# Score groups in neighbouring PSUM banks, chosen by age, and FFN outputs two units into the next block

## The chip, the cores and the metric

The kernel runs on one NeuronCore of a Trainium2 chip. The metric is the device time of one execution in microseconds, inputs in HBM to output in HBM; times are given as medians of several runs. The engines are named as the profile names them: PE (matmuls and transposes; PEld is its weight load), DVE, ACT, POOL and SP, which here only issues DMAs.

## The reference

Causal attention with a few "beacon" keys ahead of the sequence, then a feed-forward network whose hidden layer is the maximum of three products:

```python
B, H, S, Nb, D = 8, 8, 576, 16, 64
k_all = concatenate([beacon_k, k], axis=2)            # 592 keys, beacons always seen
v_all = concatenate([beacon_v, v], axis=2)
scores = q @ k_all.transpose(0, 1, 3, 2) / sqrt(D)    # masked where key is later than query
a = exp(scores - max); a /= a.sum(-1) + 1e-9
x = (a @ v_all).transpose(0, 2, 1, 3).reshape(B * S, H * D)     # 4608 x 512
h = maximum(maximum(x @ w1, x @ w2), x @ w3)          # 512 -> 768
out = h @ w_out                                       # 768 -> 512
```

All inputs and the output are float32 in HBM; the kernel computes in bfloat16 with float32 sums.

## The kernel before

The 64 heads (8 batches of 8) are worked on as 32 pairs of heads. Two pairs make a quad; two quads make a batch. The program's order is written out by hand, so each engine runs its instructions in the order in which the code emits them. Pairs 0 to 7 are emitted step by step (`first_steps` and the loop over `PPB` to `FIRST_BURST`), with PSUM banks in fixed roles. From pair 8 on each pair is one round, and all eight PSUM banks form one ring: `next_bank` takes the bank that was taken longest ago and puts it at the ring's end. This ring is where the change acts.

A round of pair p emits, in order:

- `emit_burst(p)`: the scores of both heads in four groups of matmuls (L510). Keys are the stationary side and queries the moving one; the two heads of a group go to two banks, and one exponential on ACT (L528) reads both banks and writes the tile `at_sb` in bfloat16. A burst takes all eight banks.
- In even rounds, `emit_pv_whole` for the quad of the two pairs before: the sums and the product with v (L628) into four banks. ACT copies the product to `raw` (L638, L639) and makes the reciprocal of the sums by a logarithm and an exponential (L644 to L646).
- The causal masks of this pair's `at_sb`, on POOL (L550).
- Five or six FFN units. A unit of the first product (`mm1_unit`, L703) makes 128 hidden channels of 512 tokens for one of the three weights, four matmuls into one bank, and DVE copies it (L720) or takes the maximum with what is there (L722). A unit of the output (`mm2_unit`, L750) makes 128 tokens of the output, six matmuls into one bank, and DVE copies it to `y` (L757). The last unit of a round (`close`) is cut into two halves in two banks. After the first unit, in rounds up to pair 14, stands the turn of the next pair: transposes of q and k on PE (L387) into two banks, copied by ACT (L423) and DVE (L434). Later pairs are turned by transposing DMAs instead (L379, L380). After the second unit come the plan's steps: casts of k, q and v from float32 on POOL (L260, L303), loads, stores.
- In even rounds at the end, `finish`: DVE multiplies `raw` by the reciprocal into two rows of `xT` (L651), which the first product reads.

Stores of output (L782), loads and transposing DMAs are all issued by SP, which takes them in order.

The FFN's blocks of 512 tokens are listed ahead in `units`: 18 units of the first product, then four of the output, for nine blocks. A unit may be emitted when its tokens' attention has been finished (`need` against `ready`). What is left after pair 31 runs at the end: three units, the last product, two units, the last `finish`, then the rest.

The two banks of a score group are the next two of the ring, sorted; the exponential reads them as a view with their distance as step (L522, L530):

```python
lo, hi = sorted(next_bank() for _ in range(2))
...
    in_=acc[:, lo : hi + 1 : hi - lo, 0 : g_width(p, gi)],
```

Of the kernel before, what the change touches and what calls it, by code (L numbers as in the profile page):

```python
# [16 lines left out]
def kernel(  # L17
# [23 lines left out]
    TOKB = 512  # L41
# [18 lines left out]
    PPB = H // 2  # L60
# [20 lines left out]
    NG = len(groups_any)  # L81
# [11 lines left out]
    def groups(p):  # L93
        if p < PPB:
            return groups_0
        return groups_any if p < FIRST_WHOLE else groups_whole

    def g_width(p, gi):
        return sum(q1 - q0 for _, q0, q1 in groups(p)[gi])
# [34 lines left out]
    N_BANK = 8  # L134
    acc = psum.tile([128, N_BANK, 512], FP32, name="acc")
# [18 lines left out]
    free_banks = list(range(N_BANK))  # L154

    def next_bank():
        i = free_banks.pop(0)
        free_banks.append(i)
        return i

    def next_psum(dtype=FP32):
        view = acc[:, next_bank()]
        return view if dtype == FP32 else view.bitcast(dtype)
# [32 lines left out]
    def pv_bank(i, dtype=FP32):  # L196
        return pv_psum[i].tile(dtype)
# [186 lines left out]
    def turn(p, i, ps):  # L384
        src = stage.pop(("pair16", p, i))
        for r in range(QR):
            nc.tensor.transpose(  # L387
                ps[:, r * QP : (r + 1) * QP],
                src[:, r].rearrange("p h d -> p (h d)"),
                ident[0:QP, 0:QP],  # L390
            )
# [30 lines left out]
    def evac_q(p, ps, copy):  # L422
        copy(  # L423
            qTs[p % NT].rearrange("d (p r) -> d p r", r=QR),
            ps.rearrange("d (r p) -> d p r", r=QR),
        )
# [5 lines left out]
    def evac_k(p, ps, copy):  # L432
        kT = kTs[p % NT]
        copy(  # L434
            kT[:, Nb:NK].rearrange("d (p r) -> d p r", r=QR),
            ps.rearrange("d (r p) -> d p r", r=QR),
        )
# [8 lines left out]
    def turn_pair(p, q_copy, spare="pv"):  # L446
        if spare == "any":
            banks = [next_psum(BF16) for i in range(2)]
        elif spare == "sc":
            ps = sc_psum.tile(BF16)  # L450
            banks = [ps[:, i] for i in range(2)]
        else:
            banks = [pv_bank(i, BF16) for i in range(2)]
        banks = [bank[:, 0:S] for bank in banks]
        for i in range(2):
            turn(p, i, banks[i])
        evac_k(p, banks[1], by_dve)
        evac_q(p, banks[0], q_copy)
# [21 lines left out]
    def both_heads(p, gi):  # L480
        W = g_width(p, gi)
        x0 = g_base(p, gi)
        return at[p][:, x0 : x0 + 2 * W].rearrange("k (e c) -> k e c", e=2)
# [24 lines left out]
    def score(p, t, e, q0, q1, ps):  # L508
        hs = slice(64 * e, 64 * e + 64)
        nc.tensor.matmul(  # L510
            ps,
            kTs[p % NT][hs, 128 * t : 128 * t + 128],
            qTs[p % NT][hs, q0:q1],
            start=True,
            stop=True,
            tile_position=(64 * e, 0),
        )

    def emit_burst(p):
        at[p] = at_pool.tile([128, AT_W], BF16, name="at_sb")  # L520
        for gi in range(NG):
            lo, hi = sorted(next_bank() for _ in range(2))  # L522
            off = 0
            for t, q0, q1 in groups(p)[gi]:
                for e in range(2):
                    score(p, t, e, q0, q1, acc[:, (lo, hi)[e], off : off + q1 - q0])
                off += q1 - q0
            nc.scalar.activation(  # L528
                out=both_heads(p, gi),
                in_=acc[:, lo : hi + 1 : hi - lo, 0 : g_width(p, gi)],  # L530
                func=AF.Exp,
                scale=scale,
            )
# [251 lines left out]


    units = []
    for tb in range(n_tokb):
        need = 2 * ((TOKB * (tb + 1) - 1) // S) + 1
        if tb == 0:  # L790
            for n, lo in ((0, 0), (need, MID)):
                for i in range(2):
                    for ft in range(0, n_ft, 2):
                        units.append((n, mm1_halves, (tb, ft, i, lo, lo + MID)))
        for i in range(2 if tb == 0 else 0, 3):
            for ft in range(n_ft):
                units.append((need, mm1_unit, (tb, ft, i)))
        for tt in range(TOKB // 128):
            units.append((need, mm2_unit, (tb, tt)))
    END = len(units)  # L800
    UPB = END // n_tokb
    done = [0]
# [5 lines left out]
    def emit_ffn(limit, new_ps=ffn_psum.tile, close=False):  # L808
        if not may_emit(limit):
            return False  # L810
        need, fn, args = units[done[0]]
        done[0] += 1
        fn(*args, new_ps, *([True] if close else []))
        return True
# [75 lines left out]
    def steps(p):  # L890
        return [[0, 1], [2, 3]]
# [55 lines left out]
    for b in range(2, B):  # L947
        p = b * PPB
# [5 lines left out]
    for b in range(B_PE, B):  # L954
        p = b * PPB
# [9 lines left out]
    def emit_all():  # L965
        start()
        for group, fns in first_steps:
            if group:
                emit_scores(*group)
            for fn in fns:  # L970
                fn()
        first = done[0]
        n_step = 0
        n_y = 0
        for p in range(PPB, FIRST_BURST):
            for s, gs in enumerate(steps(p)):
                for gi in gs:
                    emit_scores(p, gi)
                for gi in gs:
                    emit_masks(p, gi)  # L980
                for args in pv_at.pop((p, s), ()):
                    emit_pv(*args)
                    invert_sums()

                n_step += 1
                allowed = first + n_step * (UPB - first) / N_FIRST
                if s == 0:
                    turn_pair(p + 1, by_act, "pv" if p < PPB + 2 else "sc")
                    emit_ffn(allowed)
                    place_beacons(p + 1, by_act)  # L990
                    store_y(n_y)
                    n_y = len(y_out)
                    for fn in plan.pop((p, s), ()):
                        fn()
                    emit_ffn(allowed)
                    n_y = len(y_out)
                    emit_ffn(allowed)
                    multiply()
                else:
                    emit_ffn(allowed)  # L1000
                    multiply()
                    store_y(n_y)
                    n_y = len(y_out)
                    for fn in plan.pop((p, s), ()):
                        fn()
                    emit_ffn(allowed)
                    n_y = len(y_out)
                while emit_ffn(allowed):
                    pass
        v_tiles.pop(0)  # L1010

        for p in range(FIRST_BURST, NPAIR):
            b, pi = divmod(p, PPB)
            emit_burst(p)
            finish = emit_pv_whole(p // 2 - 1) if p % 2 == 0 else None
            for gi in range(NG):
                emit_masks(p, gi)
            n_step += 2
            if n_step <= N_FIRST:
                allowed = first + n_step * (UPB - first) / N_FIRST  # L1020
            else:
                allowed = UPB + (n_step - N_FIRST) * UPB / (2 * PPB)
            n = 0
            while may_emit(allowed):
                n_y = len(y_out)
                emit_ffn(allowed, next_psum, not may_emit(allowed, 1))
                store_y(n_y)
                n += 1
                if n == 1 and p + 1 < B_PE * PPB:
                    turn_pair(p + 1, by_act, "any")  # L1030
                    place_beacons(p + 1, by_act)
                if n == 2:
                    for fn in plan.pop((p, 0), ()):
                        fn()
            assert n >= 2
            if finish:
                finish()
            for s in range(2):
                for fn in plan.pop((p, s), ()):
                    fn()  # L1040
            if pi == 0:
                v_tiles.pop(b - 1)
        assert not plan and not loads and not pv_at
        for _ in range(3):
            emit_ffn(END, next_psum)
        finish = emit_pv_whole(NPAIR // 2 - 1)
        for _ in range(2):
            emit_ffn(END, next_psum)
        finish()
        store_y(len(y_out))  # L1050
        while emit_ffn(END - 1, next_psum):
            store_y(len(y_out))
        mm2_last(n_tokb - 1, TOKB // 128 - 1, (0, 320, 512))

    with tc.manual_schedule():
        emit_all()
# [30 lines left out]
```

## Time and profile before

| | |
|---|---|
| median of 3 runs | 329.25 us (324.11, 329.25, 329.5) |
| profiled execution | 325.05 us, span 323.3 us |
| mean granted PE clock | 0.973 |
| PE busy | 288.2 us (89%) |
| DVE, ACT, POOL busy | 182.0, 150.0, 132.9 us |
| stretch of bursts | about 58.7 to 261.8 us |
| FFN alone, after the last product | from 271.1 us |

The span is from the first to the last instruction. A wait is put down to the one that came last of what an instruction waited for, and the time in the chain of waits follows the work that ended last back to the start. A line number is that of the kernel before; in a helper all callers share it. The granted clock is given as a share of full speed.

### The profile page before, as it was taken

How to read it: one execution, taken by the hardware profiler on the slowest of the kernel's cores; microseconds unless marked ns; L12 is line 12 of the kernel's file. 1: busy time of each engine (PE TensorE's matmuls, PEld its weight loads, DVE VectorE, ACT ScalarE, POOL GpSimd, SP SyncE). 2: the span in 40 equal slices, each digit the busy share in tenths (PEclk: the TensorE clock that was granted, in tenths of full speed). 3: DMA queues.
4: the chain of work that ended last, by engine and by line, in shares of the span. 5: the costliest groups of instructions: out<-in, count | busy, mean ns of one | idle time of the engine just before them, and what ended most of it. 6: DMA issues, size and time to landing. Idle time of an engine off the chain costs nothing.

```text
span 323.3 us, 8611 instructions
## 1 busy us (share of the span) xinstructions
PE 288.2 (89%) x3539; PEld 165.1 (51%) x3539; DVE 182.0 (56%) x330; ACT 150.0 (46%) x247; POOL 132.9 (41%) x253
## 2 busy tenths in 40 slices
PE   7789969996997979968997889987998899999995
PEld 4557645554563445525553477744554455444442
DVE  4746724470946529433745437562945395776873
ACT  3775755866474274634674245547464733000000
POOL 6274674656284744462461635374225220000000
PEclk9999989997999899979998999999999999999999
DMA  8999999999864599979989699938502000301103
GB/s 153 189 178 254 216 250 265 207 299 233 211 153 90 122 277 222 151 156 253 279 182 162 161 275 205 193 110 177 113 2 97 34 2 2 130 3 65 65 1 132
DMA packets 85320, 50.67 MB, mean 157 GB/s; under 512 B 64416, under 2 KB 80032, under 8 KB 85280
## 3 DMA queue, kind: packets, MB, share of 16 engines
q1 hardware_dynamic: 80672, 45.76, 61.8%
q0 software_dynamic: 4048, 4.03, 7.5%
q8 instruction: 27, 0.44, 0.6%
q10 hardware_dynamic: 560, 0.33, 0.4%
q14 instruction: 13, 0.11, 0.1%
HBM read 35.13 MB, written 14.22 MB: 153 GB/s over the span
## 4 chain that ended last, share of the span: by engine, by line
PE 73%; ACT 9%; DMA 6%; POOL 4%; issue 3%; DVE 3%; SPq 1%; ACTq 0%; POOLq 0%; DVEq 0%
PE acc L703 39%; PE acc L750 13%; PE acc L628 10%; ACT at_sb L528 7%; PE acc L510 5%; DMA st<-in_v_dram 3%; DMA quad<-in_k_dram 2%; ACT at_sb L504 2%; POOL v_sb L303 2%; PE acc L387 1%; PE acc L594 1%; DVE hT L722 1%; POOL p L260 1%; PE acc L495 1%; SPq L222 1%
## 5 line engine op out<-in xcount | busy, mean ns | idle before, releaser
L703 PE MATMUL acc<-xT,w_sb 128*128 128x512 bf16 (+1 forms) x732 | 136.5, 342 | 0.0
L528 ACT ACTIVATE at_sb<-acc 128x416 bf16<-128x416 f32 (+1 forms) x96 | 76.1, 867 | 87.1 <-PE acc L510 56.1
L550 POOL TENSOR_SCALAR_AFFINE_SELECT at_sb<-at_sb 128x256 bf16<-128x256 bf16 (+2 forms) x148 | 58.9, 411 | 116.5 <-ACT at_sb L528 98.8
L703 PEld LDWEIGHTS <-w_sb 128*128 128x128 bf16 x732 | 69.8, 98 | 57.8 <-issue 0.8
L722 DVE TENSOR_TENSOR hT<-hT,acc 128x512 bf16<-128x512 bf16 (+1 forms) x114 | 69.8, 630 | 38.7 <-PE acc L703 36.1
L750 PE MATMUL acc<-w_out_sb,hT 128*128 128x512 bf16 (+1 forms) x246 | 53.4, 369 | 4.0 <-ACT at_sb L528 2.6
L720 DVE CAST hT<-acc 128x512 bf16<-128x512 f32 (+1 forms) x54 | 33.0, 630 | 41.5 <-PE acc L703 35.3
L260 POOL CAST p<-st 96x768 bf16<-96x768 f32 x56 | 44.4, 822 | 0.4 <-DMA st<-in_k_dram 0.4
L757 DVE COPY y<-acc 128x512 f32<-128x512 f32 (+1 forms) x41 | 25.1, 613 | 31.6 <-PE acc L750 16.3
L750 PEld LDWEIGHTS <-hT 128*128 128x128 bf16 x246 | 24.0, 102 | 29.0 <-issue 7.7
L510 PE MATMUL acc<-qT,kT 64*128 64x80 bf16 (+4 forms) x288 | 25.1, 282 | 13.1 <-ACT at_sb L528 12.5
L504 ACT ACTIVATE at_sb<-acc 128x992 bf16<-128x992 f32 (+6 forms) x32 | 26.3, 863 | 13.1 <-PE acc L495 13.0
L510 PEld LDWEIGHTS <-kT 64*128 64x128 bf16 x288 | 12.8, 94 | 27.4 <-issue 22.2
L628 PE MATMUL acc<-at_sb,v_sb 128*32 128x80 bf16 (+5 forms) x936 | 24.2, 249 | 0.0
L775 ACT COPY y<-acc 128x320 f32<-128x320 f32 x1 | 0.4, 425 | 46.3 <-PE acc L768 46.3
L651 DVE TENSOR_TENSOR xT<-raw,recip 128x576 bf16<-128x576 f32 x26 | 20.7, 838 | 0.0
L303 POOL CAST v_sb<-st 128x1536 bf16<-128x1536 f32 (+2 forms) x21 | 18.3, 893 | 1.5 <-DMA st<-in_v_dram 1.5
L638 ACT COPY raw<-acc 128x496 f32<-128x496 f32 x26 | 14.2, 597 | 9.5 <-PE acc L628 9.5
L628 PE MATMUL acc<-at_sb,ones 128*32 128x80 bf16 (+5 forms) x468 | 14.2, 248 | 5.0 <-ACT at_sb L528 5.0
L628 PEld LDWEIGHTS <-v_sb 128*32 128x32 bf16 (+1 forms) x936 | 16.2, 100 | 4.3 <-issue 0.2
L434 DVE COPY kT<-acc 128x576 bf16<-128x576 bf16 x12 | 9.0, 753 | 9.1 <-ACT kT L430 5.1
L731 PE MATMUL acc<-xT,w_sb 128*128 128x256 bf16 x96 | 13.0, 285 | 0.8 <-DVE qT L423 0.6
(65 smaller groups left out, 172.7 us busy)
## 6 DMA issues: line engine op xcount, KB each, us to landing
out_dram<-y SPq DMA_DIRECT2D x35, 256.0 KB, 2.1
st<-in_q_dram SPq DMA_DIRECT2D x28, 288.0 KB, 5.3
st<-in_k_dram SPq DMA_DIRECT2D x28, 288.0 KB, 6.1
st<-in_v_dram SPq DMA_DIRECT2D x24, 256.0 KB, 5.8
w_sb<-in_moe_w_dram POOLq DMA_DIRECT2D x6, 384.0 KB, 6.7
q_dram<-p SPq DMA_DIRECT2D x16, 144.0 KB, 2.3
k_dram<-p SPq DMA_DIRECT2D x16, 144.0 KB, 2.2
st<-in_v_dram SPq DMA_DIRECT2D x8, 224.0 KB, 5.5
```

The lines of the kernel that those rows point to most:

```text
L260: cast(t16.rearrange("p r h d -> p h r d"), st[0:QP, i * NQ2 : (i + 1) * NQ2].rearrange("p (h r d) -> p h r d", h=2, r=QR),)
L303: cast(v_sb[0:n, t:t1].rearrange("p t h d -> p (t h d)"), st[0:n, (t - t_lo) * H * D : (t1 - t_lo) * H * D],)
L504: nc.scalar.activation(out=both_heads(p, gi), in_=ps[:, :, 0 : g_width(p, gi)], func=AF.Exp, scale=scale)
L510: nc.tensor.matmul(ps, kTs[p % NT][hs, 128 * t : 128 * t + 128], qTs[p % NT][hs, q0:q1], start=True, stop=True, tile_position=(64 * e, 0),)
L528: nc.scalar.activation(out=both_heads(p, gi), in_=acc[:, lo : hi + 1 : hi - lo, 0 : g_width(p, gi)], func=AF.Exp, scale=scale,)
L550: nc.gpsimd.affine_select(out=view, in_=view, compare_op=ALU.is_ge, fill=0.0, base=x0, pattern=[[0, 2], [1, hi - lo]], channel_multiplier=-1,)
L628: nc.tensor.matmul(acc[32 * j : 32 * j + 32, bank, lo + q0 - qa : lo + qb - qa], lhsT, at_view(PPQ * quad + j // 2, t, j % 2, q0, qb), sta ...
L703: nc.tensor.matmul(ps[:, a:b], w_in[i][:, ct, 128 * ft : 128 * (ft + 1)], xT[:, ct, x0 : x0 + b - a], start=(ct == 0), stop=(ct == n_ct - 1),)
L720: by_dve(h[:, lo:hi], ps[:, lo:hi])
L722: nc.vector.tensor_max(h[:, lo:hi], h[:, lo:hi], ps[:, lo:hi])
L750: nc.tensor.matmul(ps[:, lo:hi], hT[:, ft, 128 * tt : 128 * (tt + 1)], w_out_sb[:, ft, lo:hi], start=(ft == 0), stop=(ft == n_ft - 1),)
L757: nc.vector.tensor_copy(y[:, lo:hi], ps[:, lo:hi])
```

## The change

Score groups: `next_pairs` puts the four aligned pairs of banks (0 and 1, 2 and 3, ...) in order by the later place that either bank has in the ring, and makes the ring those pairs in that order. The four groups of a burst take the pairs one after the other, and the exponential reads two neighbouring banks.

FFN order: the four output units of a block stand behind the first two units of the next block. Block 0 keeps its outputs at its own end, and so does the last one.

In pair 6 one FFN unit is emitted ahead of the next pair's turn instead of behind it.

```diff
+    def next_pairs():
+        pairs = sorted(
+            range(0, N_BANK, 2), key=lambda i: max(free_banks.index(i), free_banks.index(i + 1))
+        )
+        free_banks[:] = [i + j for i in pairs for j in range(2)]
+        return pairs
...
-        for gi in range(NG):
-            lo, hi = sorted(next_bank() for _ in range(2))
+        for gi, first in enumerate(next_pairs()):
             off = 0
             for t, q0, q1 in groups(p)[gi]:
                 for e in range(2):
-                    score(p, t, e, q0, q1, acc[:, (lo, hi)[e], off : off + q1 - q0])
+                    score(p, t, e, q0, q1, acc[:, first + e, off : off + q1 - q0])
                 off += q1 - q0
             nc.scalar.activation(
                 out=both_heads(p, gi),
-                in_=acc[:, lo : hi + 1 : hi - lo, 0 : g_width(p, gi)],
+                in_=acc[:, first : first + 2, 0 : g_width(p, gi)],
...
     units = []
+    outputs = []
     for tb in range(n_tokb):
         need = 2 * ((TOKB * (tb + 1) - 1) // S) + 1
+        blocks = []
...
         for i in range(2 if tb == 0 else 0, 3):
             for ft in range(n_ft):
-                units.append((need, mm1_unit, (tb, ft, i)))
-        for tt in range(TOKB // 128):
-            units.append((need, mm2_unit, (tb, tt)))
+                blocks.append((need, mm1_unit, (tb, ft, i)))
+        units += blocks[:2] + outputs + blocks[2:]
+        outputs = [(need, mm2_unit, (tb, tt)) for tt in range(TOKB // 128)]
+        if tb == 0:
+            units += outputs
+            outputs = []
+    units += outputs
...
                 if s == 0:
+                    if p == PPB + 2:
+                        emit_ffn(allowed)
                     turn_pair(p + 1, by_act, "pv" if p < PPB + 2 else "sc")
-                    emit_ffn(allowed)
+                    if p != PPB + 2:
+                        emit_ffn(allowed)
```

## The prediction

> **What bounds the kernel now.** I read the page first (shares, chain), then the waits of PE, then the chain in order of time, and last the granted clock in short windows.
>
> ```profile
> span 323.3 us, 8611 instructions
> PE 288.2 (89%) x3539; PEld 165.1 (51%) x3539; DVE 182.0 (56%) x330; ACT 150.0 (46%) x247; POOL 132.9 (41%) x253
> PE 73%; ACT 9%; DMA 6%; POOL 4%; issue 3%; DVE 3%; SPq 1%; ACTq 0%; POOLq 0%; DVEq 0%
> ```
>
> PE is the bound: 288.2 of 323.3 us, and 73% of the chain. So the change is worth what it takes out of PE's idle time, or out of the time that PE's own work lasts. Who makes PE wait:
>
> ```profile
> PE acc L510 <- ACT at_sb L528: 12.5, 8, 2.0
> PE acc L628 <- ACT at_sb L528: 5.0, 2, 2.5
> PE acc L750 <- ACT at_sb L528: 2.6, 1, 2.6
> PE acc L750 <- DVE hT L722: 1.4, 5, 0.3
> ```
>
> Columns: total us, times, longest. The first three rows are one thing: 8 + 2 + 1 = 11 waits, 20.1 us, all for an exponential (L528) of a burst. A burst is one head pair's scores: four groups of matmuls, each into two banks, each group read by one exponential. There are 24 bursts (pairs 8 to 31). One burst that waits, and one that doesn't (us from the start, us, what):
>
> ```profile
> 101.45 0.67 PE L510 MATMUL acc<-qT,kT 64*128 64x208 bf16 x6
> 104.10 0.43 PE L510 MATMUL acc<-qT,kT 64*128 64x336 bf16 x6 [1.98 <-ACT at_sb L528]
> 91.65 0.94 PE acc L510 x11
> 92.59 2.27 PE acc L628 x108
> ```
>
> In the burst at 101.45 the fourth group (336 columns wide at its first piece) starts 1.98 us late, released by an exponential. The burst at 91.65 takes 0.94 us and PE goes straight into the attention product.
>
> The rotation of banks says which bursts wait. Each burst begins at some place in a ring of eight banks; between bursts the kernel takes one bank for each FFN unit, a second for the last unit of the round, two for a turn, four for a product. Counted through the program, the start is odd in pairs 10, 13, 14, 17, 18, 21, 22, 25, 26, 29 and 30: eleven. With an odd start one group gets banks 7 and 0, and its view is acc[:, 0:8:7], whose reach covers all eight banks. In the instruction order of the kernel before, the matmul into bank 1 that follows carries a wait for that exponential, though it reads only 0 and 7. Eleven odd starts, eleven waits.
>
> The waits cost a second time. Where PE's granted clock was down in this stretch:
>
> ```profile
> 77.01:80.42 3.41, 3.41 (x91) 2.33 (x84) 0.00 (x0) 2.05 (x5) 1.25 (x2) 0.50 1.10 212
> 104.32:107.73 3.41, 3.41 (x22) 1.64 (x19) 0.44 (x1) 1.01 (x2) 2.27 (x5) 0.50 0.00 0
> 141.86:145.27 3.41, 3.41 (x10) 1.17 (x9) 0.69 (x1) 0.00 (x0) 3.41 (x6) 0.50 0.64 171
> 176.00:179.41 3.41, 3.31 (x13) 1.34 (x13) 0.00 (x0) 1.05 (x2) 1.99 (x4) 0.50 0.33 101
> 141.65 1.69 PE L750 MATMUL acc<-w_out_sb,hT 128*128 128x512 bf16 x4 [2.56 <-ACT at_sb L528]
> 141.65 5.73 PE acc L750 x18
> 314.40 3.88 PE acc L750 x18
> ```
>
> The value after the five engines is the clock: 0.50 for 3.41 us, four times, each within a microsecond of the end of one of the long waits. Eighteen output matmuls take 5.73 us after the wait at 141.65, against 3.88 us at the end of the kernel: 1.85 us lost.
>
> **The change, part by part.** The sum goes against the profiled execution: span 323.3, time 325.05, so 1.75 us lie around the span. That run is near the fastest shown (324.11); the median is 329.25.
>
> *Neighbouring banks.* Each group gets banks 2n and 2n+1, a view without a gap. In the instruction order after, no matmul of a burst waits for an exponential on banks other than its own. The whole 20.1 us goes. What is late next is the first bank after the burst, held by the first exponential; the burst at 91.65 shows that this is free in time. Choosing pairs by the later of their two banks can ask for a bank one place younger; the youngest stays in the last group, as before. I take 0 for it, and nothing to gain.
>
> *The clock.* Without these waits I expect the four half-clock stretches gone: 4 x 3.41 x 0.5 = 6.8 us. The drops all stand at waits of at most 2.6 us, so I count them as their price. [...]
>
> *Output units moved.* In blocks 1 to 7 the four output units (L750) now come after two units of the next block's first product (L703). That removes the wait for the last maximum (L722): 1.4 us, five times. The counts of units in each round stay as they were, and the last block's outputs stay at the end, by the instruction order. The stores of the outputs move on SP with them; the transposed fetches there are weighed below.
>
> What it adds: the first unit of a new block now stands straight behind a burst, where outputs stood, and its third and fourth matmuls read the two rows of xT that DVE is still normalising (L651).
>
> ```profile
> 85.70 1.00 PE L510 MATMUL acc<-qT,kT 64*128 64x208 bf16 x12
> 86.20 1.63 DVE L651 TENSOR_TENSOR xT<-raw,recip 128x576 bf16<-128x576 f32 x2
> 101.89 1.62 DVE L651 TENSOR_TENSOR xT<-raw,recip 128x576 bf16<-128x576 f32 x2
> 136.50 0.70 DVE hT L722
> 137.24 0.95 PE acc L750 x7
> 298.86 15.54 PE acc L703 x72
> ```
>
> Both products are done 2.06 us (103.51 - 101.45) to 2.13 us (87.83 - 85.70) after the burst's start. A matmul takes 15.54 / 72 = 0.216 us, so PE reaches the fourth at 1.00 + 3 x 0.216 = 1.65. With 0.04 us to hand over (137.20 to 137.24) that is a wait of 0.45 to 0.52; I take 0.5, in the rounds of pairs 13, 17, 21, 25 and 29: +2.5 us (at least 5 x 0.4, if the burst itself is a little longer; at most 5 x 1, if the evacuations ahead of L651 take half a microsecond more). Behind that matmul PE holds the rest of the round: the turn in round 13, the outputs and the next burst, whose exponentials and masks wait in their turn. So the wait is paid in full.
>
> At the end of attention it is longer, since block 7 follows the last product at once:
>
> ```profile
> 271.12 1.83 PE acc L703 x8
> 273.60 1.42 DVE L651 TENSOR_TENSOR xT<-raw,recip 128x576 bf16<-128x576 f32 x2
> ```
>
> PE is free at 272.95, and the last row of xT is done at 275.02. PE reaches the third matmul at 273.38 and waits for the first product (about 274.35), then for the second: the fourth starts at 275.06 instead of 273.60, +1.5 us. Before, outputs of 5.2 us covered this; that cover is gone.
>
> *A cover that the removed waits gave.* The product after burst 10 needs a cast of v on POOL:
>
> ```profile
> 72.49 1.10 PE L510 MATMUL acc<-qT,kT 64*128 64x208 bf16 x12
> 76.03 0.72 PE L628 MATMUL acc<-at_sb,ones 128*32 128x496 bf16 x16 [2.44 <-ACT at_sb L528]
> 73.77 1.17 POOL L303 CAST v_sb<-st 128x512 bf16<-128x512 f32 x2
> ```
>
> Without the 2.44 us the product starts at 73.6 and needs the cast some 0.8 us later (after 16 matmuls of sums and three key tiles); the cast ends at 74.94. +0.5 us, between 0 and 1.3.
>
> *One FFN unit ahead of the turn in pair 6.*
>
> ```profile
> 54.71 0.81 PE L387 MATMUL acc<-ident,p 96*128 96x96 bf16 x12
> 87.67 0.51 PE acc L387 x12
> 55.62 0.76 DVE L434 COPY kT<-acc 128x576 bf16<-128x576 bf16 x1 [2.90 <-PE acc L387]
> 57.17 0.60 PE L495 MATMUL acc<-qT,kT 64*128 64x496 bf16 x8
> ```
>
> This turn lasts 0.81 us where a free one takes 0.51, so a unit ahead of it can gain 0.3. It also moves the copy of kT, which frees the bank that the scores at 57.17 want, from 56.38 to about 57.25: a loss of 0 to 0.1. I take 0.
>
> *Sum.* -20.1 - 6.8 - 1.4 = -28.3; +2.5 + 1.5 + 0.5 = +4.5; together -23.8. 325.05 - 23.8 = 301.3 us. The median of the runs before stands 4.2 us above the profiled run, about what two or three more half-clock stretches of 1.7 us cost, so the median may fall a little further than the sum says.
>
> **The rivals.**
>
> *The clock stays down.* If the half-clock stretches hang on something that this change leaves, the 6.8 us remain: 301.3 + 6.8 = 308.1. For it: only four of eleven waits are followed by one, so a wait alone doesn't decide. Against: none of the four stands away from a wait. [...]
>
> *POOL becomes the bound.*
>
> ```profile
> 101.40:112.30 10.90, 8.92 (x58) 4.53 (x58) 5.59 (x9) 3.98 (x6) 7.75 (x12) 0.84 0.42 101
> 112.30:123.30 11.00, 9.02 (x161) 5.38 (x160) 4.69 (x9) 6.55 (x12) 3.41 (x7) 1.00 1.04 260
> ```
>
> The value ahead of the clock is POOL. Rounds 13 and 14 give POOL 7.75 + 3.41 = 11.2 us in 21.9. After the change they last 21.9 - 2 x 1.98 - 1.7 + 0.5 = 16.7, so POOL has room on the whole, but in the odd round nearly none. If the product in the even round waits for the last cast of v (1.17 us) in all six batches from pair 10 on, that is 7.0 in place of 0.5: 307.8.
>
> *The waits belong to the banks, not to the gapped view.* Then aligned pairs wait as well and only the output units act: 325.05 - 1.4 + 2.5 + 1.5 = 327.7, no change. Against: the thirteen bursts with an even start show no such wait.
>
> *Slower: the transposed fetches come late.*
>
> ```profile
> SPq L782 <- DVE y L757: 108.8, 23, 25.3
> 111.02 1.20 SPq L380 DMA_TRANSPOSE kT<-k_dram  x1
> kT<-k_dram SPq DMA_TRANSPOSE x16, 3.5
> qT<-q_dram SPq DMA_TRANSPOSE x16, 4.6
> 128.77 0.94 PE acc L510 x11
> ```
>
> SP works in order and sits on waits of stores for outputs (L782) for 108.8 us; the change puts a block's four stores closer together, ahead of fetches. The fetch of pair 16's kT is issued by 112.22, lands about 115.7 and is read at 128.77: 13 us to spare, some 11 in the shorter rounds. From there on it decides: if SP is held 11 us longer, the first pair of each of four batches waits for both landings, 4 x (4.6 + 3.5) = 32.4, and the time is 333.7. Against: four output units last 5.2 us, half of the spare time.
>
> **How the numbers follow.** My forecast (the waits and their clock go, small new waits come) has 0.70, and is 301.3 us; its own bounds are 297.9 (xT term at 2.0, the wait at the end and that for the cast covered, the turn 0.3 shorter, each slow stretch worth 1.85 rather than 1.7: 301.3 - 0.5 - 1.5 - 0.5 - 0.3 - 0.6) and 304.6 (xT term at 5.0, cast at 1.3: + 2.5 + 0.8). The clock that stays has 0.13 (308.1), POOL 0.10 (307.8), no effect 0.04 (327.7), slower 0.03 (333.7). The first three cases hold 0.93, so the range is 297.5 to 308.5. Faster by over 2% (about what a measurement of this kernel can tell from no change): 0.93; within 2%: 0.04; slower: 0.03.
>
> **What would show it.** In the profile after: the waits of the scores, the product and the outputs for an exponential of a burst, 20.1 us in all, fall under 1 us; the granted clock between 60 and 250 us is 0.99 or 1.00; the wait of outputs for the last maximum is gone; in its place stand five waits of first-product matmuls for the normalisation of xT of about 0.5 us, one of 1.0 and one of 0.5 near the end, and one of the product for the cast of v near 73 us. PE's busy time falls by about 6.8 us, since slow matmuls count as busy. It is wrong if PE still waits over 5 us for exponentials, if half-clock stretches of 3.41 us remain without a long wait before them, or if the product waits for POOL in each batch.

## The result and the profile after

The changed kernel takes 300.9 us (median of four runs, 299.54 to 305.01) against 329.04 us: ratio 0.919, interval 0.908 to 0.930. (The ratio, here and below, compares only the fast runs of both kernels, those within 1.5% of the kernel's fastest, and so is not the quotient of the two medians, which are of all runs.) The kernel before was run again beside the experiments, with medians of 327.01 and 326.74 us; their ratios are to these runs. The profiled run takes 301.9 us, 1.7 of it around the span. The page after:

```profile
span 300.2 us, 8579 instructions
PE 282.3 (94%) x3511; PEld 163.2 (54%) x3539; DVE 180.9 (60%) x330; ACT 148.0 (49%) x247; POOL 132.7 (44%) x253
PE 78%; DMA 9%; DVE 5%; issue 2%; POOL 2%; SPq 1%; ACT 1%; POOLq 0%
```

PE still bounds the kernel, now at 94%. The waits of PE after (total us, times, longest; the code stands six or seven lines lower, so L709 is the first product, L517 the scores of the bursts, L502 those of the pairs ahead of them, L657 the normalisation of xT):

```profile
PE acc L709 <- DVE xT L657: 3.3, 7, 1.0
PE acc L502 <- ACT at_sb L511: 2.2, 5, 0.8
PE acc L517 <- ACT at_sb L511: 0.6, 1, 0.6
```

The eleven waits for a burst's exponential, 20.1 us, are gone; the 0.6 us that is left for the scores stands in both kernels and belongs to the first burst. The wait of outputs for the last maximum has no row any more. What is new is the first row, seven waits for xT.

The stretches of the two kernels (length; busy us of PE, PEld, DVE, ACT, POOL; then the granted clock, the DMA share and GB/s), before and then after:

```profile
0.00:58.70 58.70, 49.34 (x795) 31.46 (x796) 32.53 (x91) 35.20 (x58) 31.88 (x66) 0.97 1.08 214
58.70:323.30 264.60, 238.83 (x2747) 133.61 (x2746) 149.50 (x240) 114.80 (x190) 101.02 (x188) 0.97 0.62 144
```

```profile
0.00:59.80 59.80, 51.23 (x791) 31.87 (x793) 31.71 (x91) 35.16 (x58) 31.80 (x65) 0.91 1.01 205
59.80:248.00 188.20, 184.48 (x2505) 109.94 (x2527) 114.52 (x190) 112.37 (x189) 100.86 (x188) 1.00 0.84 187
248.00:300.20 52.20, 46.58 (x218) 21.35 (x219) 34.69 (x51) 0.43 (x1) 0.00 (x0) 1.00 0.16 61
```

From the first burst to the end the clock is 1.00, where it was 0.97. From the first burst's start to the end the span falls from 264.7 to 240.4 us, by 24.3; the stretch ahead of it is 1.1 us longer, at a clock of 0.91 against 0.97. That stretch differs from run to run in every kernel here, so from now on two numbers are given: the median of the time, and "the rest", from the first burst's start (the first matmul of the helper `score`) to the end of the span.

Where the 24.3 us went, from the starts of PE's matmuls (each line is given the time from its matmul's start to the next one's start, from the first burst on):

| | before | after | neighbouring pairs alone (below) |
|---|---|---|---|
| scores | 44.3 | 23.8 | 23.5 |
| first product | 127.9 | 131.6 | 127.4 |
| outputs | 52.6 | 46.0 | 48.3 |
| product with v | 30.7 | 29.6 | 29.8 |
| turns | 3.9 | 3.8 | 3.6 |

The scores lose 20.5 us. (A wait counts with the line ahead of it.) The outputs take 6.6 us less and the product with v 1.1, mostly because the slow matmuls behind the waits are gone (4.3 and 0.9 us less with the pairs alone). The first product takes 3.7 us more.

### The profile page after: what moved, and what is told of

Its sections match the earlier page's. It is cut to its first block, busy times and chain, and to the rows that moved or that the text cites. A ratio compares the mean times of both kernels' runs of the same rounds, so it can differ in the third digit from the quotient of the medians.

```text
span 300.2 us, 8579 instructions
## 1 busy us (share of the span) xinstructions
PE 282.3 (94%) x3511; PEld 163.2 (54%) x3539; DVE 180.9 (60%) x330; ACT 148.0 (49%) x247; POOL 132.7 (44%) x253
## 4 chain that ended last, share of the span: by engine, by line
PE 78%; DMA 9%; DVE 5%; issue 2%; POOL 2%; SPq 1%; ACT 1%; POOLq 0%
PE acc L709 41%; PE acc L756 15%; PE acc L634 10%; DMA st<-in_v_dram 8%; PE acc L517 6%; DVE xT L657 3%; PE acc L600 2%; DVE hT L728 2%; PE acc L394 2%; ACT at_sb L511 1%; PE acc L502 1%; DMA h<-in_q_dram 1%; SPq L229 1%; POOL v_sb L310 1%; PE acc L737 1%
## 5 line engine op out<-in xcount | busy, mean ns | idle before, releaser
L709 PE MATMUL acc<-xT,w_sb 128*128 128x512 bf16 (+1 forms) x709 | 135.5, 340 | 4.5 <-DVE xT L657 3.3
L534 ACT ACTIVATE at_sb<-acc 128x416 bf16<-128x416 f32 (+1 forms) x96 | 75.3, 868 | 69.3 <-PE acc L517 58.5
L709 PEld LDWEIGHTS <-w_sb 128*128 128x128 bf16 x732 | 69.1, 98 | 59.8 <-issue 4.4
L556 POOL TENSOR_SCALAR_AFFINE_SELECT at_sb<-at_sb 128x256 bf16<-128x256 bf16 (+2 forms) x148 | 58.7, 411 | 89.9 <-ACT at_sb L534 71.6
L756 PE MATMUL acc<-w_out_sb,hT 128*128 128x512 bf16 (+1 forms) x241 | 46.8, 347 | 0.2
L517 PE MATMUL acc<-qT,kT 64*128 64x80 bf16 (+4 forms) x288 | 24.7, 280 | 0.6 <-ACT at_sb L511 0.6
L634 PE MATMUL acc<-at_sb,v_sb 128*32 128x80 bf16 (+5 forms) x936 | 23.2, 243 | 0.0
L657 DVE TENSOR_TENSOR xT<-raw,recip 128x576 bf16<-128x576 f32 x26 | 20.7, 839 | 0.0
L517 PEld LDWEIGHTS <-kT 64*128 64x128 bf16 x288 | 12.4, 94 | 15.0 <-issue 10.7
L502 PE MATMUL acc<-qT,kT 64*128 64x288 bf16 (+7 forms) x112 | 11.1, 287 | 2.2 <-ACT at_sb L511 2.2
```

Of the source, the lines that this page charges most:

```text
L517: nc.tensor.matmul(ps, kTs[p % NT][hs, 128 * t : 128 * t + 128], qTs[p % NT][hs, q0:q1], start=True, stop=True, tile_position=(64 * e, 0),)
L534: nc.scalar.activation(out=both_heads(p, gi), in_=acc[:, first : first + 2, 0 : g_width(p, gi)], func=AF.Exp, scale=scale,)
L556: nc.gpsimd.affine_select(out=view, in_=view, compare_op=ALU.is_ge, fill=0.0, base=x0, pattern=[[0, 2], [1, hi - lo]], channel_multiplier=-1,)
L634: nc.tensor.matmul(acc[32 * j : 32 * j + 32, bank, lo + q0 - qa : lo + qb - qa], lhsT, at_view(PPQ * quad + j // 2, t, j % 2, q0, qb), sta ...
L657: nc.vector.tensor_mul(xT[:, 2 * g + i, c0 : c0 + S], raw[:, i], recip)
L709: nc.tensor.matmul(ps[:, a:b], w_in[i][:, ct, 128 * ft : 128 * (ft + 1)], xT[:, ct, x0 : x0 + b - a], start=(ct == 0), stop=(ct == n_ct - 1),)
```

## The experiments

### The pairs alone

The kernel before with `next_pairs` and nothing else of the change:

```diff
-            lo, hi = sorted(next_bank() for _ in range(2))
+        for gi, first in enumerate(next_pairs()):
...
-                in_=acc[:, lo : hi + 1 : hi - lo, 0 : g_width(p, gi)],
+                in_=acc[:, first : first + 2, 0 : g_width(p, gi)],
```

> Neighbouring pairs alone; the FFN list and pair 6 as before. Theory (the gapped view's reach made the waits, and the moved outputs cost more than they give): no wait of PE for a burst's exponential; the waits for the normalisation of xT after bursts (1.95 us in the changed kernel's profile) and at the end (1.31 us) are gone, the five waits of outputs for the last maximum (1.4 us) are back. Against the changed kernel: -3.3 + 1.4 = -1.9 us, median about 299.0 us, 9% under before. Rival (the two edits need each other, the outputs' move carries part of the gain): 303 us or more.

Measured: 300.75 us (six runs; ratio 0.923, 0.919 to 0.927). The rest is 237.8 us, 2.5 shorter than in the changed kernel. Its waits of PE:

```profile
PE acc L502 <- ACT at_sb L511: 2.4, 5, 0.9
PE acc L394 <- POOL p L267: 2.0, 2, 1.5
PE acc L600 <- POOL at_sb L556: 1.5, 1, 1.5
PE acc L756 <- DVE hT L728: 1.4, 5, 0.3
```

No wait for a burst's exponential and none for xT; the five waits for the last maximum are back. So the pairs carry the whole gain, and in the profile the moved outputs cost 2.5 us of it. The median, 1.75 us above the 299.0 expected, does not show that: the stretch before the bursts was 61.3 us here against 59.8. By the table the move adds 4.2 us to the first product (131.6 - 127.4) and takes 2.3 from the outputs, +1.9 of the 2.5; the scores' 0.3 is another part of it. Both are more than the idle rows say (3.3 and 1.4): rows of matmuls overlap when nothing waits (before, a matmul of 512 columns in the first product has a row of 0.38 us, while the matmuls start 0.216 us apart), so each wait costs some 0.15 us on top of its idle time (4.2 - 3.3 over seven, 2.3 - 1.4 over five).

### The same banks, the gapped exponential made as two

The kernel before; where a group has banks 0 and 7, one exponential per bank:

```diff
+            if hi - lo == 1:
...
+            else:
+                for e in range(2):
+                    nc.scalar.activation(
+                        out=both_heads(p, gi)[:, e],
+                        in_=acc[:, (lo, hi)[e], 0 : g_width(p, gi)],
...
```

> The kernel before, with the exponential over banks 0 and 7 (one group in eleven bursts) made as two, one for each bank; all else, the order of banks too, is as before. Theory (reach of the gapped view): the eleven waits of 20.1 us go and the half-clock stretches behind them too, so it comes within 1.5 us of neighbouring pairs alone: about 299 to 301 us, though ACT has eleven instructions more. Rival (what counts is which banks are taken, by age and alignment): the waits stay, 325 to 329 us.

Measured: 299.93 us (four runs; ratio 0.920, 0.914 to 0.927), the rest 237.5 us. The waits of PE that are left in the rest:

```profile
PE acc L759 <- DVE hT L731: 1.4, 5, 0.3
PE acc L510 <- ACT at_sb L504: 0.6, 1, 0.6
```

A burst that had waited 1.98 us (its exponentials on ACT, then the PE rows):

```profile
100.06 1.35 ACT L529 ACTIVATE at_sb<-acc 128x416 bf16<-128x416 f32 x2 [3.63 <-issue]
101.30 1.07 ACT L537 ACTIVATE at_sb<-acc 128x496 bf16<-128x496 f32 x2
102.22 1.03 ACT L529 ACTIVATE at_sb<-acc 128x992 bf16<-128x992 f32 x1
```

```profile
99.70 0.95 PE L510 MATMUL acc<-qT,kT 64*128 64x208 bf16 x12
100.63 1.46 PE L759 MATMUL acc<-w_out_sb,hT 128*128 128x512 bf16 x5
```

Twelve matmuls in 0.95 us, then the outputs. The order of banks by age is the one of before, bank for bank; only the view's reach is gone. That settles the cause: the reach of the view made the waits, not which banks were taken. The eleven more instructions on ACT (L537, two in 1.07 us, where one over both banks takes 1.01 us by its mean in the kernel before) cost PE nothing.

### A wider reach in every group

The changed kernel with banks n and n + 4:

```diff
-        pairs = sorted(
-            range(0, N_BANK, 2), key=lambda i: max(free_banks.index(i), free_banks.index(i + 1))
-        )
-        free_banks[:] = [i + j for i in pairs for j in range(2)]
+        pairs = sorted(
+            range(4), key=lambda i: max(free_banks.index(i), free_banks.index(i + 4))
+        )
+        free_banks[:] = [i + j for i in pairs for j in (0, 4)]
...
-                in_=acc[:, first : first + 2, 0 : g_width(p, gi)],
+                in_=acc[:, first : first + 5 : 4, 0 : g_width(p, gi)],
```

> The changed kernel with banks n and n + 4 for a group in place of 2n and 2n + 1, so every group's view spans five banks. Theory (reach): in the instruction order 96 matmuls now wait for an exponential of other banks, four in each of 24 bursts, so each burst runs at the pace of ACT, about 2.0 to 2.6 us longer: +48 to +62 us, and half-clock stretches beside them, 350 to 375 us. Rival (what counts is the order of banks by age): no more than 3 us from the changed kernel.

Measured: 448.77 us (two runs; ratio 1.374, 1.362 to 1.387); the rest 385.4 us, 145 us longer than in the changed kernel. The direction is that of the theory, the size was far too small. The waits, one burst of it, and two stretches of the clock:

```profile
PE acc L517 <- ACT at_sb L534: 69.7, 72, 1.2
PE acc L634 <- ACT at_sb L534: 8.7, 8, 1.1
PE acc L709 <- ACT at_sb L534: 6.5, 6, 1.1
...
PE acc L756 <- ACT at_sb L534: 1.1, 1, 1.1
```

```profile
74.52 0.26 PE L517 MATMUL acc<-qT,kT 64*128 64x208 bf16 x2
75.73 0.37 PE L517 MATMUL acc<-qT,kT 64*128 64x464 bf16 x2 [0.95 <-ACT at_sb L534]
77.14 0.71 PE L517 MATMUL acc<-qT,kT 64*128 64x496 bf16 x3 [1.03 <-ACT at_sb L534]
78.69 0.57 PE L517 MATMUL acc<-qT,kT 64*128 64x336 bf16 x5 [0.84 <-ACT at_sb L534]
80.34 2.72 PE L756 MATMUL acc<-w_out_sb,hT 128*128 128x512 bf16 x6 [1.08 <-ACT at_sb L534]
```

```profile
61.10:446.50 385.40, 293.98 (x2747) 152.41 (x2746) 148.69 (x240) 124.33 (x190) 101.27 (x188) 0.84 0.42 100
77.30:84.20 6.90, 4.97 (x28) 2.33 (x25) 0.83 (x2) 2.62 (x4) 4.48 (x8) 0.51 0.19 68
```

The waits are 72 + 8 + 6 + 1 = 87 and 86.0 us: 3.6 us in each of 24 bursts, since scores and exponentials take turns, each group waiting about one exponential (0.84 to 1.08 us in the burst shown; in the kernel before an exponential over 128x992 takes 1.01 us, one over 128x928 0.94). I had expected 2.0 to 2.6 us a burst, the pace of ACT, and left out that every exponential itself starts only after its group's late matmuls. The other part is the clock, 0.84 over the whole rest: 0.16 x 385 = 62 us at most, since PE is idle in part of the slow stretches. 86 + 62 = 148 holds the 145. By the starts of PE's matmuls the scores, with which these waits count, take 101.5 us more than in the changed kernel, and the other lines 43.5 us more.

### The outputs' move alone

The kernel before with the new list of `units` and the old banks (the second part of the diff).

> The moved outputs alone, banks and pair 6 as before. The move takes one unit out of each even round that ends a block and puts it into the odd round behind it, which turns five odd starts of the ring even: by count, gapped views remain in six bursts (pairs 10, 14, 18, 22, 26, 30) instead of eleven. Theory: the waits of those six stay (11.3 us by before's trace: 2.44, 1.98, 1.01, 2.52, 1.99, 1.31), 8.8 us go, with one or more half-clock stretches; the waits for the normalisation of xT come (3.3 us) and those for the last maximum go (1.4 us): 313 to 319 us. Rival (the move is worth its own terms alone, +1.9 us): 327 to 331 us.

Measured: 319.17 us (four runs; ratio 0.975, 0.966 to 0.984), the rest 253.5 us. Its waits, and the one half-clock stretch in the rest:

```profile
PE acc L510 <- ACT at_sb L528: 6.3, 4, 2.0
PE acc L628 <- ACT at_sb L528: 5.0, 2, 2.5
PE acc L703 <- DVE xT L651: 3.3, 7, 1.0
```

```profile
214.90:218.30 3.40, 3.40 (x98) 2.25 (x87) 0.00 (x0) 1.89 (x5) 2.22 (x4) 0.50 1.09 114
```

Six waits, 11.3 us, and one slow stretch, 1.7 us: together 13.0, and the rest is 13.1 us above that of the changed kernel. The median stands just above the 313 to 319 us that were expected; in the profiled run (321.13 us) the first burst starts only at 65.9 us. So the move, alone, is worth more than its own terms, by a side effect: it shifts the ring's parity. With aligned pairs there is no parity left to shift, and what remains of the move is its cost.

### The normalisation issued earlier

The changed kernel with DVE's two multiplications into xT ahead of the unit that closes an even round (and, after the last product, one unit earlier too):

```diff
                 n_y = len(y_out)
+                if finish and not may_emit(allowed, 1):
+                    finish()
                 emit_ffn(allowed, next_psum, not may_emit(allowed, 1))
...
```

> The changed kernel, but DVE's two multiplications into xT (the normalisation) are issued ahead of the last unit of an even round rather than behind it, and at the end ahead of the last unit before them. Theory: the five waits of the new block's first unit go (1.95 us) and the one at the end falls from 1.31 to under 0.5 us: about 298 to 298.5 us. Rival (DVE's copies of the last units come 1.6 us later, and the burst waits for their banks instead): the time stays at 300.9 us.

Measured: 313.25 us (six runs; ratio 0.961, 0.955 to 0.967). Neither came true; the rival had the right mechanism, and it costs four times what it saves (11.1 us of new waits against 2.8). The profile is of the longest run, 317.06 us, whose first burst starts at 62.5 us; its rest is 252.7 us, 12.3 more than in the changed kernel. The waits, and one burst on DVE and PE:

```profile
PE acc L517 <- DVE hT L730: 11.1, 11, 1.1
PE acc L502 <- ACT at_sb L511: 2.4, 6, 0.8
...
PE acc L711 <- DVE xT L657: 0.5, 2, 0.3
```

```profile
86.23 1.42 DVE L657 TENSOR_TENSOR xT<-raw,recip 128x576 bf16<-128x576 f32 x2
87.57 0.74 DVE L730 TENSOR_TENSOR hT<-hT,acc 128x256 bf16<-128x256 bf16 x2
```

```profile
86.39 0.66 PE L517 MATMUL acc<-qT,kT 64*128 64x208 bf16 x5
88.03 0.72 PE L517 MATMUL acc<-qT,kT 64*128 64x496 bf16 x7 [0.98 <-DVE hT L730]
```

The five waits of new blocks for xT are gone (0.5 us is left, at the end). But in DVE's order the closing unit's two maxima (L730, from 87.57) now stand behind the multiplications (from 86.23), and the next burst's third group wants their banks. That is 0.98 us in the burst shown, and it comes after every even round, not only where a block begins. The wait for xT was real, but removing it by DVE's order costs more than it saves.

### The pairs, with closing outputs interleaved

Neighbouring pairs, outputs in their old place, and in an output unit that closes a round the last hidden tile comes last for both halves:

```diff
-        for lo, hi in parts(end):
-            ps = new_ps()
-            for ft in range(n_ft):
+        cuts = [(lo, hi, new_ps()) for lo, hi in parts(end)]
+        for fts in (range(n_ft - 1), range(n_ft - 1, n_ft)):
+            for lo, hi, ps in cuts:
+                for ft in fts:
...
```

> Neighbouring pairs, outputs where they were before, and in an output unit that closes a round the matmuls of the last hidden tile of both halves come after those of the first five of both (so the wait for the last maximum, 0.29 us five times, is covered by 0.5 us more of matmuls). Theory: 1.4 us under neighbouring pairs alone, about 297.6 us. Rival (the copies of both halves now come late together, and the next burst waits for its last banks): the same as neighbouring pairs alone, or up to 5 x 0.5 us more.

Measured: 299.15 us (six runs; ratio 0.920, 0.914 to 0.925). The waits for the last maximum are gone, none for xT has come, and the rest is 236.8 us: 1.0 under the pairs alone, where 1.4 was expected, and 3.5 under the changed kernel. The rival is there in part: by starts the outputs take 2.2 us less than with the pairs alone (48.3 to 46.1) and the scores 1.3 more (23.5 to 24.8). The six bursts behind such an output unit last 0.2 to 0.3 us longer; in the one at 128.59 us of the second profile below, the sixth matmul starts 0.18 us behind the fifth, released by DVE's copy of y, where with the pairs alone the two start together. These delays are too short for a row of waits. Once more, beside the changed kernel:

> Neighbouring pairs, outputs in their old place, closing output halves interleaved, once more. Theory: from the first burst's start to the end it is 3.5 us shorter than the changed kernel (236.8 against 240.4 us in the profiles), so its median comes out 2 to 4 us under it if the stretch before the bursts is alike on average. Rival: the stretch before the bursts varies by as much as that and the medians agree within 1 us.

> The changed kernel, beside the next one on the same chip. Theory: its time from the first burst's start to the end is 240.4 us again, with waits for xT of 3.3 us in all; the median is 300 to 302 us.

Measured: 302.2 us (297.77 to 304.42, ratio 0.924, 0.917 to 0.931) and, for the changed kernel, 300.87 us (299.02 to 304.63, ratio 0.920, 0.914 to 0.926), six runs each. The rests repeat to 0.1 us: 236.8 and 240.4. The medians do not tell the two apart, and in this pair they even stand the other way round. What hides the 3.5 us is the stretch before the bursts, which only the edit in pair 6 touches, and that without effect (see below):

| kernel, profiled run | first burst starts | rest | half-clock stretches before it, us |
|---|---|---|---|
| before | 58.7 | 264.7 | 3.4 |
| changed | 59.8 | 240.4 | 10.2 |
| changed, again | 58.2 | 240.4 | 3.4 |
| pairs alone | 61.3 | 237.8 | 6.8 |
| pairs, interleaved | 64.5 | 236.8 | 13.7 and 6.8 |
| pairs, interleaved, again | 59.2 | 236.8 | 3.4 |

So the interleaved version is better from the first burst on in both profiles, and as a whole kernel it is not shown to be faster than the changed one.

## Why the prediction was right, step by step

- The eleven waits (20.1 us to go): right. They are gone here and in the split version, where nothing but the reach differs; with more reach there are 87.
- The clock (6.8 us to go): right, and this decides the rival that kept the slow stretches at 308.1. No such stretch lies between the first burst and the last 4 us in any version without waits for a burst's exponential (the clock is 1.00 there in the changed kernel, with the pairs alone, with the split exponential, with the early normalisation and in the second profile of the interleaved pairs). Between before and the pairs alone, the lines other than the scores take less time by 4.3 (outputs), 0.9 (product), 0.5 (first product) and 0.3 us (turns): 6.0 us, with some more in the scores.
- The wait for the last maximum (1.4 us to go): it went, and was worth 2.3 us.
- The new waits for xT (2.5 us in five rounds, 1.5 at the end): there, at the rounds named. One of the five, and the end:

```profile
96.82 1.02 PE L517 MATMUL acc<-qT,kT 64*128 64x208 bf16 x12
97.77 0.82 PE L709 MATMUL acc<-xT,w_sb 128*128 128x512 bf16 x3
99.02 0.38 PE L709 MATMUL acc<-xT,w_sb 128*128 128x512 bf16 x1 [0.42 <-DVE xT L657]
97.34 1.63 DVE L657 TENSOR_TENSOR xT<-raw,recip 128x576 bf16<-128x576 f32 x2
249.28 0.38 PE L709 MATMUL acc<-xT,w_sb 128*128 128x512 bf16 x1 [1.02 <-DVE xT L657]
249.95 1.24 PE L709 MATMUL acc<-xT,w_sb 128*128 128x512 bf16 x5 [0.29 <-DVE xT L657]
```

  Three matmuls run, the fourth is 0.42 us late, released when L657 ends at 98.97. By idle time 2.0 + 1.3 = 3.3 us, by starts 4.2: the 4.0 lies between.
- The cast of v after burst 10 (0.5 us to come): wrong, it cost nothing.

```profile
74.68 0.72 PE L634 MATMUL acc<-at_sb,ones 128*32 128x496 bf16 x16
74.94 1.17 POOL L310 CAST v_sb<-st 128x512 bf16<-128x512 f32 x2
75.22 1.25 PE L634 MATMUL acc<-at_sb,v_sb 128*32 128x496 bf16 x32
```

  PE runs on without a gap. The row is two casts of 0.61 us; I took the end of both, and the fourth key tile needs only the first, which ends at 75.55, while that tile is read from 75.60 on. PE had 0.05 us to spare.
- The unit ahead of pair 6's turn (0): right. From the product ahead of the turn to the first burst's second group, before and then after:

```profile
53.16 1.61 PE acc L594 x76
59.53 0.80 PE acc L510 x10
```

```profile
54.31 1.61 PE acc L600 x76
60.69 0.80 PE acc L517 x10
```

  59.53 - 53.16 = 6.37 and 60.69 - 54.31 = 6.38.
- "The counts of units in each round stay as they were": wrong. The next block's units may not be emitted before its tokens are ready, so each even round that ends a block has one unit fewer and the odd round behind it one more. In the changed kernel this moves nothing that can be seen; with the old banks it is worth five gapped views, as the outputs' move alone shows.
- POOL as the bound, and late fetches: neither shows. POOL is busy 100.9 of 188.2 us in the stretch of bursts, and PE has no row of waits for it or for a DMA there.

The sum was 4.5 us of new waits against 28.3 removed. Measured from the first burst on it is 24.3 net against 23.8; the stretch before it, 1.1 us longer in this profile, brings the profiled run to 301.9 against 301.3 predicted. That the whole comes within 0.6 us is in part luck. The mechanisms were right, but some of their sizes were not: about 0.4 us too much for the clock, 0.9 too little for the last maximum, 0.5 for a cast that cost nothing; these misses partly cancel. And the stretch before the bursts, which the sum took as it was, differs by 1.7 us between two profiles of the changed kernel.

## What to carry to other kernels

In this kernel two banks read by one instruction through a stepped view held all the banks between them, in the waits that the program carries (eleven waits and 20.1 us with banks 7 and 0 in one group of eleven bursts, 87 and 86.0 us with banks n and n + 4 in every group): count the parity of a ring that hands out pairs, since one extra buffer taken elsewhere decides whether the gap appears. Splitting the one instruction that spans the gap, or taking neighbours, was worth the same here (a rest of 237.5 and 237.8 us). When a wait is removed, price the other edits again without it: the outputs' move was worth 2.5% by itself, and in the profiles from the first burst on it turned into a loss of 2.5 us beside the pairs.

## What the runs showed of the hardware

In the kernel before, five half-clock stretches begin at 46.29, 77.01, 104.32, 141.86 and 176.00 us; each lasts 3.41 us at a clock of 0.50, and their starts lie 30.72, 27.31, 37.54 and 34.14 us apart, 9, 8, 11 and 10 times 3.41. A last one, from 322.77, is cut off by the end of the record. In the changed kernel there is one, of 10.24 us from 17.92, three times 3.41. I counted PE's idle time in the trace of the kernel before, up to 319.36 us, in steps of 3.41 us that fit these starts. The five steps ahead of a drop hold 1.87, 1.98, 2.17, 2.43 and 2.56 us of idle time, and the steps with most idle time and no drop behind them hold 1.86, 1.61 and 1.48. So in that trace the drops stand behind the steps with most idle time, but no limit is shown: between a step with a drop behind it and one without lies 0.01 us. The wait of 2.52 us that ends at 187.27 in the kernel before has no drop behind it; the two steps that it straddles hold 1.48 and 1.03 us. This fits with only four of eleven waits being followed by one. The length of single waits does not sort the runs either: with the early normalisation eleven waits of about 1.0 us each leave the clock at 1.00 from 62.5 to 312 us, and with banks four apart, where no wait is longer than 1.2 us, it is 0.84 over the rest. (In the first stretch the count of idle time doesn't explain the drops: the one at 17.92 in the changed kernel follows a step with 1.02 us of idle time, less than the 1.86 us that have none behind them in the kernel before.) What makes the clock fall is not shown.

That first stretch is the other thing I had not expected: in versions without any edit in it, it holds from 3.4 to 20.5 us of half clock in the profiles of the table above. And in the two kernels that were profiled twice it makes the whole difference between the two profiles, 1.7 us for the changed kernel and 5.3 us for the interleaved pairs. What brings it about is open.
